# Second stage of an attention and feed-forward kernel: seven products of quarters in place of eight

## The chip, the cores and the metric

The kernel runs on one core of a Trainium2 chip. The metric is the device time of one execution in microseconds (us), the median of several runs. The profile is of one execution; its engines are PE (TensorE matmul), PEld (its weight loads), DVE (VectorE), ACT (ScalarE), POOL (GpSimd) and SP (SyncE, which issues DMAs here).

## The reference

A decayed attention over 2 batches, 8 heads, 768 positions and 64 channels gives x of 1536 tokens by 512. Then come a normalization and two feed-forward stages in float32:

```python
xn = x / np.sqrt(np.mean(x * x, axis=-1, keepdims=True) + 1e-06) * rms_g
g = xn @ w_gate                                  # 512 x 1536
y = (g * (1.0 / (1.0 + np.exp(-g))) * (xn @ w_val)) @ w_out
h = np.maximum(np.maximum(y @ w1, y @ w2), y @ w3)   # 512 x 768 each
out = h @ w_out2
```

Call the line of y the first stage, the last two lines the second.

## The kernel before

**Tiles.** Tokens are columns, cut into NBLK=3 blocks j of 512. The contraction of 512 is cut into KD=4 slices of 128. The width of the first stage is 12 tiles f of 128, that of the second 6. `feed_forward` (L427) goes through a list of steps (stage, group, j, f): within a group of f (groups1 = 4, 2, 2, 2, 2; groups2 = 2, 2, 2) over the three blocks j, and within j over the f. A step makes a hidden tile (`hidden1` L384: the products pg and pv, sigmoid, two multiplications; `hidden2` L396: three products pw0 to pw2, one ACT copy, two DVE maxima), cuts it (`split`), and while PE goes on, the step before it is multiplied by its rows of the output weight (`out1`, `out2`) into four PSUM banks `acc`. At a group's end `drain1` or `drain2` adds these to a sum in SBUF; at the end of the last group of the first stage `drain1` also cuts y into yh and yl. PSUM has 8 banks of 128x512, all from one pool.

**Float32 by three products.** `mm3` (L336) does each 128x128 by 128x512 product as three matmuls: high by high, high weight by low data, low weight by high data. A high part is a cast to fp32r on ACT, the low part source minus high: `split` (L349) puts the cast (hh, L350) on ACT and the subtraction (hl, L351) on POOL.

**Weights.** A weight tile of 512 columns (a unit: name g, v, o of the first stage; 1, 2, 3, p of the second; and f) arrives as 64-bit words in the tile `wraw` by a DMA from SP, three in flight. `make_unit` (L142) turns it into wh and wl over three calls, each of which advances three units at once: ACT does an absolute value and a scaling of the raw words (L173, L174); a call later DVE does three operations (L153, L155, L157: `W`) and POOL one integer addition (L159); a call later ACT casts wh (L148) and POOL subtracts wl (L149). All instructions stand in the order in which the Python code issues them. `gap` (L323) is called after each 6 matmuls of the products and the output products, and makes every fourth of these calls a `make_unit` in both stages' main part. So what stands behind what in an engine's queue is set by where `gap` falls.

```python
        pos["gap"] += 1
        if (pos["gap"] + 5) % (2 if pos["step"] < groups1[0] else 4) == 0:
            make_unit()
```

Of the kernel before, what the change touches and what calls it, by code (L numbers as in the profile page):

```python
# [18 lines left out]
P = 128  # L19
# [7 lines left out]
def tile_decay_attention_swiglu_maxout(  # L27
# [23 lines left out]
    NB = 512  # L51
    WBUFS = 12
# [12 lines left out]
    wpools = [wp]  # L65

# [42 lines left out]
    unit_list = [(nm, f) for f in range(F1) for nm in "gvo"] + [(nm, f) for f in range(F2) for nm in "123p"]  # L109
    groups1, groups2 = [4, 2, 2, 2, 2], [2, 2, 2]  # L110
    group_of = {}
    for n0, groups, names in ((0, groups1, "gvo"), (len(groups1), groups2, "123p")):
        f0 = 0
        for g_, n_ in enumerate(groups):
            group_of.update({(nm, f): n0 + g_ for nm in names for f in range(f0, f0 + n_)})
            f0 += n_
    steps = []
    for stage_, groups in ((1, groups1), (2, groups2)):
        f0 = 0
        for g_, n_ in enumerate(groups):  # L120
# [21 lines left out]
    def make_unit():  # L142

        if len(stage2):
            key, W, at = stage2.pop(0)
            wh = wpools[at].tile([P, 512], F32R, tag="wh", name="wh")
            wl = wpools[at].tile([P, 512], F32R, tag="wl", name="wl")
            nc.scalar.copy(out=wh, in_=W.bitcast(F32))  # L148
            nc.gpsimd.tensor_tensor(out=wl, in0=W.bitcast(F32), in1=wh.bitcast(F32), op=ALU.subtract)  # L149
            units[key] = (wh, wl)  # L150
        if len(stage1):
            key, W, at, lo, hi = stage1.pop(0)
            nc.vector.tensor_scalar(out=W.bitcast(F32), in0=W.bitcast(F32), scalar1=LEAST, scalar2=MOST,  # L153
                                    op0=ALU.max, op1=ALU.min)
# [10 lines left out]
        if first_use[key] <= pos["step"] + 6 and at < len(wpools) and room[at]:  # L165
            load_to(pos["made"] + (3 if pos["step"] else 1))
            room[at] -= 1
            held[key] = at
            pos["made"] += 1
            t = raws.pop(key).rearrange("p k (f w) -> p (k f) w", w=2)  # L170
            lo, hi = t[:, :, 0], t[:, :, 1]
            W = wp.tile([P, 512], I32, tag="W", name="W", bufs=3)
# [150 lines left out]
    def gap():  # L323
# [17 lines left out]
    def proj(ps, unit, bh, bl):  # L341
        wh, wl = unit
        for kk in range(KD):
            ks = slice(kk * P, (kk + 1) * P)
# [10 lines left out]
    yb = {}  # L355

    def drain1(acc, g, j):
        if g == 0:
# [3 lines left out]
            return  # L362
        for m in range(KD):
            nc.vector.tensor_tensor(out=acc_sb[j][:, m, :], in0=acc[m], in1=acc_sb[j][:, m, :], op=ALU.add)
        if g == len(groups1) - 1:
            yh = act.tile([P, KD, NB], F32R, tag="xh", name="yh", bufs=3)
            yl = act.tile([P, KD, NB], F32R, tag="xl", name="yl", bufs=3)
            for m in range(KD):
                split(yh[:, m, :], yl[:, m, :], acc_sb[j][:, m, :])
            yb[j] = (yh, yl)  # L370

    def drain2(acc, g, j):
        if g == 0:
            acc_sb[j] = act.tile([P, KD, NB], F32, tag="acc", name="acc_sb", bufs=3)
        for t in range(KD):
            if g == 0:
                nc.scalar.copy(out=acc_sb[j][:, t, :], in_=acc[t])
                continue
            nc.vector.tensor_tensor(out=acc_sb[j][:, t, :], in0=acc[t], in1=acc_sb[j][:, t, :], op=ALU.add)
            if g == len(groups2) - 1:  # L380
                r0 = j * NB + t * P
                nc.sync.dma_start(out=out[r0:r0 + P, :], in_=acc_sb[j][:, t, :])

    def hidden1(f, j):  # L384
# [4 lines left out]
        proj(pv, units["v", f], bh, bl)  # L389
# [5 lines left out]

    def hidden2(f, j):  # L396
        bh, bl = yb[j]
        ps = []
        for i in range(3):
            pw = bank(f"pw{i}")  # L400
            proj(pw, units["123"[i], f], bh, bl)
            ps.append(pw)
        m1 = act.tile([P, NB], F32, tag="sg", name="m1", bufs=1)
        nc.scalar.copy(out=m1, in_=ps[0])
        nc.vector.tensor_tensor(out=m1, in0=ps[1], in1=m1, op=ALU.max)  # L405
        nc.vector.tensor_tensor(out=m1, in0=ps[2], in1=m1, op=ALU.max)
        return m1
# [9 lines left out]
    def out2(acc, f, f0, f1, hh, hl):  # L417
        wh, wl = units["p", f]
        for t in range(NB // P):
            ts = slice(t * P, (t + 1) * P)  # L420
            nc.tensor.matmul(out=acc[t], lhsT=hh[:, ts], rhs=wh, start=f == f0, stop=False)  # L421
            nc.tensor.matmul(out=acc[t], lhsT=hh[:, ts], rhs=wl, start=False, stop=False)  # L422
            nc.tensor.matmul(out=acc[t], lhsT=hl[:, ts], rhs=wh, start=False, stop=f == f1)  # L423
            if t % 2:
                gap()

    def feed_forward():  # L427
        acc = []
        before = None
        for now in steps + [None]:  # L430
            if now:
                pos["step"] = steps.index(now)
                stage, g, j, f, f0, f1 = now
                if stage == 1 and g == 0 and f == f0:
# [7 lines left out]
                r = (hidden1 if stage == 1 else hidden2)(f, j)  # L442
                hh = act.tile([P, NB], F32R, tag="hh", name="hh")
                hl = act.tile([P, NB], F32R, tag="hl", name="hl")
                split(hh, hl, r)
            if before:
                stage, g, j, f, f0, f1, ph, pl = before
                if f == f0:
                    acc = [bank("acc") for _ in range(4)]
                (out1 if stage == 1 else out2)(acc, f, f0, f1, ph, pl)  # L450
                if f == f1:
                    (drain1 if stage == 1 else drain2)(acc, g, j)
                if j == NBLK - 1:
                    for nm in ("gvo" if stage == 1 else "123p"):
                        del units[nm, f]
                        room[held.pop((nm, f))] += 1
            if now:
                before = (*now, hh, hl)
# [64 lines left out]
```

## Time and profile before

| | us |
|---|---|
| median of 3 runs (lowest, highest) | 581.58 (581.4, 581.93) |
| the profiled execution | 582.03 |
| its span in the profile | 580.2 |
| PE busy in the span | 563.9 |
| DVE busy | 341.4 |
| ACT busy | 223.4 |
| POOL busy | 292.7 |
| mean granted TensorE clock | 0.996 |

The span is what the profiler saw of the core's instructions; the execution's own time holds what lies around it as well. Busy time is the time in which an engine ran an instruction, and PE's part of it holds all the kernel's matmuls. Tiles of the second stage are called pw, m, hh, hl and acc in the rows, those of the first pg, pv, sg, hh, hl and acc; the hidden tile of the second stage uses the buffer of sg.

### The profile page before, as it was taken

The page shows a single profiled execution, that of the slowest core. Times are in us where ns is not written, and L with a number is a line of the kernel's source. Part 1 is how long each engine was busy: PE and PEld are TensorE (multiplying, and loading weights), DVE is VectorE, ACT ScalarE, POOL GpSimd, SP SyncE. Part 2 cuts the span into 40 slices and gives each one's busy share as a digit, 9 for nine tenths or more (in the row PEclk, how much of TensorE's full clock was granted, in tenths as well). Part 3 has the DMA queues.
Part 4 walks back from the last instruction along what each step waited for, and adds up shares of the span by engine and source line. Part 5 has one row for each costly group of instructions (what it writes and reads, how often), then busy time and mean ns, then how long its engine had stood idle before and what let it go on. Part 6 is the DMA issues. An engine that isn't in the chain of part 4 may idle for free.

```text
span 580.2 us, 7727 instructions
## 1 busy us (share of the span) xinstructions
PE 563.9 (97%) x2970; PEld 466.5 (80%) x2970; DVE 341.4 (59%) x467; ACT 223.4 (38%) x422; POOL 292.7 (50%) x231
## 2 busy tenths in 40 slices
PE   7979898999999999999999999999999999999997
PEld 7868676888788888888888888888888888888885
DVE  6687996433556783775477388868732674321322
ACT  3656653432453642342253245553532533101100
POOL 2577988211356773365256257988741566110110
PEclk9998999999999999999999999999999999999999
DMA  9677554000033231132033022322321220000111
GB/s 213 169 194 193 143 163 128 1 2 0 2 108 110 73 108 37 36 104 78 0 111 105 4 72 73 109 74 73 108 73 37 69 77 2 0 0 1 74 72 73
DMA packets 64645, 44.54 MB, mean 77 GB/s; under 512 B 39264, under 2 KB 60768, under 8 KB 64608
## 3 DMA queue, kind: packets, MB, share of 16 engines
q1 hardware_dynamic: 63936, 44.05, 25.8%
q8 instruction: 23, 0.38, 0.3%
q14 instruction: 14, 0.11, 0.1%
q10 hardware_dynamic: 672, 0.01, 0.1%
HBM read 40.90 MB, written 3.15 MB: 76 GB/s over the span
## 4 chain that ended last, share of the span: by engine, by line
PE 87%; DVE 7%; DMA 2%; ACT 2%; issue 1%; SPq 0%; POOL 0%; DVEq 0%; ACTq 0%
PE pw L339 8%; PE pw L337 8%; PE pw L338 8%; PE acc L337 5%; PE pv L337 5%; PE pg L337 5%; PE pg L338 5%; PE pv L339 5%; PE acc L339 5%; PE pg L339 5%; PE acc L338 5%; PE pv L338 5%; PE acc L423 3%; PE acc L421 3%; PE acc L422 3%; PE px L244 2%
## 5 line engine op out<-in xcount | busy, mean ns | idle before, releaser
L149 POOL TENSOR_TENSOR wl<-W,wh 128x512 fp32r<-128x512 f32 x60 | 90.7, 1511 | 21.1 <-ACT wh L148 21.1
L351 POOL TENSOR_TENSOR hl<-sg,hh 128x512 fp32r<-128x512 f32 x36 | 47.3, 1314 | 101.3 <-ACT hh L350 98.4
L159 POOL TENSOR_TENSOR W<-W,wraw 128x512 int32<-128x512 int32 x60 | 80.1, 1335 | 17.9 <-DVE W L157 13.0
L157 DVE SCALAR_TENSOR_TENSOR W<-wraw,W 128x512 int32<-128x512 int32 x60 | 84.3, 1405 | 2.1
L337 PE MATMUL pw<-yh,wh 128*128 128x512 f32 x216 | 84.0, 389 | 0.0
L338 PE MATMUL pw<-yl,wh 128*128 128x512 f32 x216 | 84.0, 389 | 0.0
L339 PE MATMUL pw<-yh,wl 128*128 128x512 f32 x216 | 84.0, 389 | 0.0
L351 POOL TENSOR_TENSOR hl<-m,hh 128x512 fp32r<-128x512 f32 x18 | 23.3, 1294 | 102.3 <-ACT hh L350 102.3
L392 DVE TENSOR_TENSOR sg<-pg,sg 128x512 f32<-128x512 f32 x36 | 24.7, 687 | 60.2 <-ACT sg L391 60.2
L337 PE MATMUL pv<-xh,wh 128*128 128x512 f32 x144 | 57.1, 397 | 1.0 <-DVE x L300 1.0
L337 PE MATMUL pg<-xh,wh 128*128 128x512 f32 x144 | 58.0, 403 | 0.1
L148 ACT CAST wh<-W 128x512 fp32r<-128x512 f32 x60 | 37.2, 619 | 54.4 <-POOL W L159 54.3
L338 PE MATMUL pg<-xl,wh 128*128 128x512 f32 x144 | 56.7, 394 | 0.5 <-DVE xl L311 0.5
L339 PE MATMUL pg<-xh,wl 128*128 128x512 f32 x144 | 56.7, 394 | 0.3 <-POOL wl L149 0.3
L337 PE MATMUL acc<-hh,wh 128*128 128x512 f32 x144 | 56.9, 395 | 0.0
L350 ACT CAST hh<-sg 128x512 fp32r<-128x512 f32 x36 | 22.4, 622 | 88.9 <-DVE sg L393 88.9
L339 PE MATMUL pv<-xh,wl 128*128 128x512 f32 x144 | 56.2, 390 | 0.0
L339 PE MATMUL acc<-hh,wl 128*128 128x512 f32 x144 | 56.1, 390 | 0.0
L338 PE MATMUL acc<-hl,wh 128*128 128x512 f32 x144 | 56.1, 390 | 0.0
L338 PE MATMUL pv<-xl,wh 128*128 128x512 f32 x144 | 56.1, 390 | 0.0
L405 DVE TENSOR_TENSOR m<-pw,m 128x512 f32<-128x512 f32 x18 | 12.4, 691 | 70.6 <-PE pw L339 59.8
L153 DVE TENSOR_SCALAR W<-W 128x512 f32<-128x512 f32 x60 | 42.6, 710 | 9.2 <-POOL hl L351 4.8
(84 smaller groups left out, 1063.3 us busy)
## 6 DMA issues: line engine op xcount, KB each, us to landing
wraw<-in_moe_w_out_dram SPq DMA_DIRECT2D x18, 512.0 KB, 3.3
wraw<-in_moe_w_dram SPq DMA_DIRECT2D x18, 512.0 KB, 3.5
wraw<-in_moe_w_gate_dram SPq DMA_DIRECT2D x12, 512.0 KB, 3.6
wraw<-in_moe_w_val_dram SPq DMA_DIRECT2D x12, 512.0 KB, 3.6
kn<-in_k_dram SPq DMA_DIRECT2D x12, 256.0 KB, 4.0
qn<-in_q_dram SPq DMA_DIRECT2D x12, 256.0 KB, 4.4
vn<-in_v_dram SPq DMA_DIRECT2D x12, 256.0 KB, 4.7
out_dram<-acc_sb SPq DMA_DIRECT2D x12, 256.0 KB, 2.1
```

The costliest lines, as they stand in the source:

```text
L148: nc.scalar.copy(out=wh, in_=W.bitcast(F32))
L149: nc.gpsimd.tensor_tensor(out=wl, in0=W.bitcast(F32), in1=wh.bitcast(F32), op=ALU.subtract)
L153: nc.vector.tensor_scalar(out=W.bitcast(F32), in0=W.bitcast(F32), scalar1=LEAST, scalar2=MOST, op0=ALU.max, op1=ALU.min)
L157: nc.vector.scalar_tensor_tensor(out=W, in0=hi, scalar=-0x40000000, in1=W, op0=ALU.bitwise_and, op1=ALU.bitwise_or)
L159: nc.gpsimd.tensor_tensor(out=W, in0=W, in1=lo, op=ALU.add)
L337: nc.tensor.matmul(out=out, lhsT=wh, rhs=xh_, start=first, stop=False)
L338: nc.tensor.matmul(out=out, lhsT=wh, rhs=xl_, start=False, stop=False)
L339: nc.tensor.matmul(out=out, lhsT=wl, rhs=xh_, start=False, stop=last)
L350: nc.scalar.copy(out=dst_h, in_=src)
L351: nc.gpsimd.tensor_tensor(out=dst_l, in0=src, in1=dst_h.bitcast(F32), op=ALU.subtract)
L392: nc.vector.tensor_tensor(out=sg, in0=pg, in1=sg, op=ALU.mult)
L421: nc.tensor.matmul(out=acc[t], lhsT=hh[:, ts], rhs=wh, start=f == f0, stop=False)
```

## The change

The first stage's steps stay, except for their end. The second stage is written anew, as a list of pieces.

**Seven products for eight.** For a pair of f (three pairs g) and each of w1, w2, w3 (i), the blocks j=0 and j=1 and the two halves of the contraction make a two by two matrix of quarters, as do the pair of f and the halves of the weight. Their product takes eight products of quarters (6 matmuls of 128x512 each). The change does it in Strassen's way, in Winograd's form, with seven. They need sums of quarters of y (s1 to s4, made once) and of the weights (T1, T2, T3, per pair and made in place in `W` by four DVE subtractions of 128x256, L174, then cast and cut like any unit: 18 more units of cast and low half). Block j=2 stays plain: four pieces of 6 matmuls per pair and weight. So a pair and weight takes 11 pieces, 66 matmuls, where it took 72.

**Banks.** The products 1, 6, 7 and 4 accumulate one after another into one bank `p`, 5 and 3 into a bank `r`, 2 into `q`. Between them ACT copies the state of the bank to SBUF (`held_back`: c1, u2, m5), and DVE adds that copy to another bank (`add_max`): for i=0 one addition, for i=1, 2 an addition and a maximum of two SBUF tiles. `just_max` is one ACT copy (i=0) or one DVE maximum with a bank.

**Placing.** `first_stage` runs out1 of (f=11, j=1) early, in the middle of pv of (f=10, j=2) (`early`), and its `drain1` leaves two of four sums in PSUM; `sums_of_quarters` puts six pieces of work into `later`, and each `gap` pops one. T1, T2 of the first pair and the units 1, 2, 3 of it are made in the first stage. The last out1 (f=11, j=2) stands behind two pieces of the second stage (`second_stage`). `gap` makes a unit after pieces 5, 2 and 7, and after every second token tile of out2, which now stands once per pair, for all three j.

```diff
+    unit_list = [(nm, f) for f in range(F1) for nm in "gvo"]
+    unit_list += [("1", 0), ("1", 1), None, ("T1", 0), ("T1", 1), ("2", 0), ("2", 1), None, ("T2", 0), ("T2", 1),
+                  ("3", 0), ("3", 1)]
...
+            elif key and key[1] % 2 == 0:
+                a, b = W.bitcast(F32), words[key[0][1], key[1] + 1].bitcast(F32)
+                for o, x, y in ((a[:, :HF], b[:, :HF], a[:, :HF]), (b[:, :HF], b[:, HF:], b[:, :HF]),
+                                (b[:, HF:], b[:, HF:], a[:, :HF]), (a[:, HF:], a[:, HF:], b[:, HF:])):
+                    nc.vector.tensor_tensor(out=o, in0=x, in1=y, op=ALU.subtract)
...
+        keep = g == len(groups1) - 1 and j == 1
+        for m in (0, 2, 1, 3) if keep else range(KD):
+            nc.vector.tensor_tensor(out=acc[m] if keep and m < 2 else y[:, m, :], in0=acc[m], in1=y[:, m, :], op=ALU.add)
...
+        if keep:
+            sums_of_quarters(list(acc), y)
+            return
...
+        def cut(nm, k, src, eng):
+            h_, l_, o = Y[nm]
+            nc.scalar.copy(out=h_[:, o + k, :], in_=src)
+            lower(eng, h_[:, o + k, :], l_[:, o + k, :], src)
+
+        def one(k):
+            s3[k] = wpools[1].tile([P, NB], F32, tag=("wh", "wl")[k], name="sums")
+            nc.vector.tensor_tensor(out=s3[k], in0=y0[:, k, :], in1=ps[k], op=ALU.subtract)
+            nc.vector.tensor_tensor(out=ps[k], in0=ps[k], in1=y[:, 2 + k, :], op=ALU.add)
+            cut("s1", k, ps[k], nc.vector)
+
+        def two(k):
+            s4 = wpools[1].tile([P, NB], F32, tag=("wh", "wl")[k], name="sums")
+            nc.vector.tensor_tensor(out=ps[2 + k], in0=ps[k], in1=y0[:, k, :], op=ALU.subtract)
+            nc.vector.tensor_tensor(out=s4, in0=y0[:, 2 + k, :], in1=ps[2 + k], op=ALU.subtract)
+            cut("s2", k, ps[2 + k], nc.vector)
+            cut("s4", k, s4, nc.gpsimd)
+
+        def three(k):
+            cut("s3", k, s3[k], nc.gpsimd)
+            cut("22", k, y[:, 2 + k, :], nc.gpsimd)
+
+        for k in range(2):
+            later.extend([lambda k=k: one(k), lambda k=k: two(k), lambda k=k: three(k)])
...
+    def add_max(ps, c, i, key, n):
+
+        if i == 0:
+            nc.vector.tensor_tensor(out=hidden_tile(key, n), in0=ps, in1=c, op=ALU.add)
+            return
+        nc.vector.tensor_tensor(out=c, in0=ps, in1=c, op=ALU.add)
+        nc.vector.tensor_tensor(out=hid[key], in0=hid[key], in1=c, op=ALU.max)
+        if i == 2:
+            halves(key)
...
+        if n == 1:
+            ps_of[at, "p"] = p = bank("p")
+            product(p, u0, 0, Y["11"], True)
+            ps_of[at, "c1"] = held_back(p, "wh")
...
+        elif n == 6:
+            product(ps_of[at, "p"], t1, 1, Y["s2"], False)
+            ps_of[at, "u2"] = held_back(ps_of[at, "p"], "wl")
...
+        elif n == 2:
+            q_ = bank("q")
+            product(q_, u0, 1, Y["12"], True)
+            add_max(q_, ps_of.pop((at, "c1")), i, (0, 0), 2)
...
+        gap(n in (5, 2, 7))
...
+        work = [(first, 1), (first, 2), halve, finish, (first, 5), (first, 6), (second, 1), (first, 3), (first, 7),
+                (second, 2), (first, (0, 0)), (first, 4), (second, 5), (first, (0, 1)), (second, 6), (first, (1, 0)),
+                (second, 3), (first, (1, 1)), (second, 7), (second, (0, 0)), (second, (0, 1)), (second, 4),
+                (second, (1, 0)), (second, (1, 1))]
+        for g in range(F2 // 2):
+            for i in range(3):
+                if g or i == 2:
+                    work += [((g, i), n) for n in (1, 5, (0, 0), 6, 2, (0, 1), 3, 7, (1, 0), (1, 1), 4)]
+                if g and i == 0:
+                    work.append(lambda g=g: out2(g - 1))
+        work.append(lambda: out2(F2 // 2 - 1))
```

**Place 1: POOL at the end of the first stage, before.** hl_3415 is the low half of the last hidden tile of the first stage, (f=11, j=2); wl_3442 and W_3447 belong to units of the second stage; yl_3516 are the low halves of y of block 2.

```order
L351 TENSOR_TENSOR hl_3415<-sg_3410,hh_3414 128x512 [waits Activation_49]
L149 TENSOR_TENSOR wl_3442<-W_3353,wh_3441 128x512 [waits Activation_49]
L159 TENSOR_TENSOR W_3447<-W_3447,wraw_3305 128x512 [waits DMAHW2_49,DVE_49,Activation_49]
L351 TENSOR_TENSOR hl_3496<-m1_3491,hh_3495 128x512 [waits Activation_49]
L351 TENSOR_TENSOR yl_3516<-acc_sb_1939,yh_3515 128x512 [waits Activation_49] x4
```

And now: hl_3449 is that same low half. xl1, xl2 and al hold the sums of quarters, W_3423 is a unit of the second pair, yl_3511 are the low halves of y of block 2.

```order
L390 TENSOR_TENSOR xl2_3368<-sums_3397,xh2_3367 128x512 [waits DVE_49,Activation_49]
L390 TENSOR_TENSOR xl1_3366<-sums_3377,xh1_3365 128x512 [waits Activation_49]
L390 TENSOR_TENSOR al_3370<-acc_sb_1671,ah_3369 128x512 [waits Activation_49]
L390 TENSOR_TENSOR xl2_3368<-sums_3437,xh2_3367 128x512 [waits DVE_49,Activation_49]
L390 TENSOR_TENSOR xl1_3366<-sums_3426,xh1_3365 128x512 [waits Activation_49]
L390 TENSOR_TENSOR al_3370<-acc_sb_1671,ah_3369 128x512 [waits Activation_49]
L169 TENSOR_TENSOR W_3423<-W_3423,wraw_3229 128x512 [waits DMAHW0_49,DVE_49]
L383 TENSOR_TENSOR hl_3449<-sg_3444,hh_3448 128x512 [waits PE_49,Activation_49,Pool_49]
L383 TENSOR_TENSOR yl_3511<-acc_sb_1942,yh_3510 128x512 [waits Activation_49] x4
```

The last hidden tile's low half stands behind six low halves of sums and behind the addition for W_3423.

**Place 2: DVE at the same place, before.** sg_3410 is the last hidden tile of the first stage, acc_sb_1668 the sum of block 1, m1_3491 the first hidden tile of the second stage.

```order
L364 TENSOR_TENSOR acc_sb_1668<-acc_3276,acc_sb_1668 128x512 [waits PE_49]
L364 TENSOR_TENSOR acc_sb_1668<-acc_3277,acc_sb_1668 128x512 [waits PE_49]
L153 TENSOR_SCALAR W_3353<-W_3353 128x512 [waits Activation_49,Pool_49]
L155 TENSOR_SCALAR W_3353<-W_3353 128x512 [waits DVE_49]
L157 SCALAR_TENSOR_TENSOR W_3353<-wraw_3255,W_3353 128x512 [waits DMAHW1_49,DVE_49]
L392 TENSOR_TENSOR sg_3410<-pg_3376,sg_3410 128x512 [waits Activation_49,Pool_49]
L393 TENSOR_TENSOR sg_3410<-pv_3389,sg_3410 128x512 [waits DVE_49,PE_49]
L153 TENSOR_SCALAR W_3447<-W_3447 128x512 [waits Activation_49,Pool_49]
L155 TENSOR_SCALAR W_3447<-W_3447 128x512 [waits DVE_49]
L157 SCALAR_TENSOR_TENSOR W_3447<-wraw_3305,W_3447 128x512 [waits DMAHW2_49,DVE_49]
L405 TENSOR_TENSOR m1_3491<-pw1_3456,m1_3491 128x512 [waits PE_49,Activation_49]
L406 TENSOR_TENSOR m1_3491<-pw2_3469,m1_3491 128x512 [waits DVE_49,PE_49]
```

And now: acc_3301 to acc_3304 are the banks of the early out1 with the sums of block 1, sg_3444 the hidden tile (11, j=2), q_3479 the second piece of the second stage.

```order
L437 TENSOR_TENSOR sums_3426<-acc_sb_1337,acc_3302 128x512
L438 TENSOR_TENSOR acc_3302<-acc_3302,acc_sb_1671 128x512
L390 TENSOR_TENSOR xl1_3366<-acc_3302,xh1_3365 128x512 [waits Activation_49]
L443 TENSOR_TENSOR acc_3304<-acc_3302,acc_sb_1337 128x512
L444 TENSOR_TENSOR sums_3437<-acc_sb_1337,acc_3304 128x512 [waits DVE_49]
L390 TENSOR_TENSOR xl2_3368<-acc_3304,xh2_3367 128x512 [waits Activation_49]
L465 TENSOR_TENSOR sg_3444<-pg_3390,sg_3444 128x512 [waits Activation_49]
L466 TENSOR_TENSOR sg_3444<-pv_3414,sg_3444 128x512 [waits DVE_49,PE_49]
L553 TENSOR_TENSOR m_3486<-q_3479,c_3477 128x512 [waits PE_49,Activation_49]
L163 TENSOR_SCALAR W_3423<-W_3423 128x512
L165 TENSOR_SCALAR W_3423<-W_3423 128x512 [waits DVE_49]
L167 SCALAR_TENSOR_TENSOR W_3423<-wraw_3229,W_3423 128x512 [waits DMAHW0_49,DVE_49]
```

The sums of the second quarter tile stand ahead of the last hidden tile's two multiplications, and the conversion of W_3423 stands behind the addition m_3486, which waits for PE's q_3479. The first matmul into q_3479 waits for the row of xl2 from acc_3304.

**Place 3: ACT where pair 0 ends and pair 1 begins, before.** The step of the second stage that makes m1_3491 (its copy and cast), then the cut of y and units.

```order
L404 COPY m1_3491<-pw0_3434 128x512 [waits PE_49,Pool_49]
L350 CAST hh_3495<-m1_3491 128x512 [waits DVE_49]
L350 CAST yh_3515<-acc_sb_1939 128x512 [waits DVE_49] x4
L148 CAST wh_3532<-W_3447 128x512 [waits Pool_49]
L173 ACTIVATE W_3542<-wraw_3445 128x512 [waits DMAHW4_49,Activation_49]
L174 ACTIVATE wraw_3445<-wraw_3445 128x512
L148 CAST wh_3571<-W_3482 128x512 [waits Pool_49]
L173 ACTIVATE W_3581<-wraw_3480 128x512 [waits DMAHW5_49,Activation_49]
```

And now: hh2_3835, hh2_3853 and hh2_3864 are casts of finished hidden tiles of pair 0 (m_3568, m_3670, m_3614), c_3875 and c_3884 the copies of the banks p and r of the first two products of pair 1.

```order
L157 CAST wh_3822<-W_3747 128x512 [waits Pool_49]
L197 ACTIVATE W_3832<-wraw_3745 128x512 [waits DMAHW5_49,Activation_49]
L198 ACTIVATE wraw_3745<-wraw_3745 128x512
L382 CAST hh2_3835<-m_3568 128x512 [waits DVE_49]
L382 CAST hh2_3853<-m_3670 128x512 [waits DVE_49]
L382 CAST hh2_3864<-m_3614 128x512 [waits DVE_49]
L577 COPY c_3875<-p_3868 128x512 [waits PE_49]
L577 COPY c_3884<-r_3877 128x512 [waits PE_49]
```

The copy that lets piece 6 of pair 1 overwrite its bank stands behind the casts of three hidden tiles, which wait for DVE. DVE reaches m_3670 and m_3614 there only behind three operations on W_3784:

```order
L555 TENSOR_TENSOR c_3739<-p_3723,c_3739 128x512 [waits PE_49]
L556 TENSOR_TENSOR m_3568<-m_3568,c_3739 128x512 [waits DVE_49]
L163 TENSOR_SCALAR W_3784<-W_3784 128x512 [waits Activation_49]
L165 TENSOR_SCALAR W_3784<-W_3784 128x512 [waits DVE_49]
L167 SCALAR_TENSOR_TENSOR W_3784<-wraw_3596,W_3784 128x512 [waits DMAHW4_49,DVE_49]
L564 TENSOR_TENSOR m_3670<-p2_3839,m_3670 128x512 [waits PE_49]
L564 TENSOR_TENSOR m_3614<-p_3723,m_3614 128x512 [waits PE_49]
```

## Rows read from the trace of the kernel before

**Rows 1.** The page, part 1: engine, busy us (share of the span) xinstructions.

```profile
PE 563.9 (97%) x2970; PEld 466.5 (80%) x2970; DVE 341.4 (59%) x467; ACT 223.4 (38%) x422; POOL 292.7 (50%) x231
```

**Rows 2.** The page, part 2: 40 slices, PE busy and granted clock in tenths.

```profile
PE   7979898999999999999999999999999999999997
...
PEclk9998999999999999999999999999999999999999
```

**Rows 3.** One window of the second stage: busy us of each engine, PEclk, DMA share, GB/s.

```profile
500.00:550.00 50.00, 50.00 (x223) 41.39 (x222) 12.36 (x18) 5.44 (x10) 5.16 (x4) 1.00 0.06 21
```

**Rows 4.** The tile pw, then the timeline's end: start us, us, engine, line.

```profile
L337 PE MATMUL pw<-yh,wh x216: 389/389/389, 377.7 to 570.1; 128*128 128x512 f32 x108
...
575.83 0.39 PE L422 MATMUL acc<-wl,hh 128*128 128x512 f32 x1
...
576.06 0.39 PE L423 MATMUL acc<-wh,hl 128*128 128x512 f32 x1
```

**Rows 5.** Groups by line and shape: busy us, mean ns of one, idle before.

```profile
L405 DVE TENSOR_TENSOR m<-pw,m 128x512 f32<-128x512 f32 x18 | 12.4, 691 | 70.6 <-PE pw L339 59.8 <-ACT m L404 10.7
...
L391 ACT ACTIVATE sg<-pg 128x512 f32<-128x512 f32 x36 | 21.3, 591 | 43.3 <-PE pg L339 43.3
...
L350 ACT CAST hh<-m 128x512 fp32r<-128x512 f32 x18 | 11.2, 622 | 73.0 <-DVE m L406 73.0
...
L404 ACT COPY m<-pw 128x512 f32<-128x512 f32 x18 | 10.4, 580 | 33.1 <-PE pw L339 33.1
...
L173 ACT ACTIVATE W<-wraw 128x512 f32<-128x512 f32 x60 | 40.1, 668 | 0.0
...
L351 POOL TENSOR_TENSOR hl<-m,hh 128x512 fp32r<-128x512 f32 x18 | 23.3, 1294 | 102.3 <-ACT hh L350 102.3
...
L159 POOL TENSOR_TENSOR W<-W,wraw 128x512 int32<-128x512 int32 x60 | 80.1, 1335 | 17.9 <-DVE W L157 13.0 <-ACT m L404 1.6 <-ACT wraw L174 1.6
```

**Rows 6.** Lines 311, 153, 155, 157 on DVE: duration min/median/max in ns.

```profile
L311 DVE TENSOR_TENSOR xl<-x,xh x4: 681/693/967, 112.9 to 148.2; 128x512 fp32r<-128x512 f32 x4
...
L153 DVE TENSOR_SCALAR W<-W x60: 411/419/1516, 24.9 to 484.6; 128x512 f32<-128x512 f32 x60
...
L155 DVE TENSOR_SCALAR W<-W x60: 426/428/1421, 25.3 to 485.0; 128x512 int32<-128x512 int32 x60
...
L157 DVE SCALAR_TENSOR_TENSOR W<-wraw,W x60: 691/1726/1811, 26.5 to 485.5; 128x512 int32<-128x512 int32 x60
```

**Rows 7.** Timeline near 362 us, DVE and POOL alone: start us, us, line.

```profile
361.11 1.38 DVE L153 TENSOR_SCALAR W<-W 128x512 f32<-128x512 f32 x1
...
362.16 1.47 POOL L149 TENSOR_TENSOR wl<-W,wh 128x512 fp32r<-128x512 f32 x1
...
362.52 1.39 DVE L155 TENSOR_SCALAR W<-W 128x512 int32<-128x512 int32 x1
...
363.95 1.67 DVE L157 SCALAR_TENSOR_TENSOR W<-wraw,W 128x512 int32<-128x512 int32 x1
```

**Rows 8.** Timeline, DVE and ACT: four free operations, two dependent ones, a handover.

```profile
371.66 1.88 DVE L364 TENSOR_TENSOR acc_sb<-acc,acc_sb 128x512 f32<-128x512 f32 x3
...
400.94 0.69 DVE L405 TENSOR_TENSOR m<-pw,m 128x512 f32<-128x512 f32 x1 [1.78 <-ACT m L404]
...
401.74 0.69 DVE L406 TENSOR_TENSOR m<-pw,m 128x512 f32<-128x512 f32 x1
...
402.46 0.62 ACT L350 CAST hh<-m 128x512 fp32r<-128x512 f32 x1 [1.61 <-DVE m L406]
```

**Rows 9.** Windows of half a microsecond in the first stage: columns as in Rows 3.

```profile
40.50:41.00 0.50, 0.00 (x0) 0.00 (x0) 0.50 (x3) 0.21 (x1) 0.22 (x1) 1.00 1.28 283
...
43.00:43.50 0.50, 0.50 (x5) 0.40 (x4) 0.50 (x1) 0.18 (x2) 0.50 (x1) 0.77 1.05 239
...
43.50:44.00 0.50, 0.50 (x3) 0.40 (x2) 0.50 (x1) 0.50 (x2) 0.27 (x1) 0.50 1.05 238
...
46.50:47.00 0.50, 0.50 (x5) 0.49 (x4) 0.50 (x1) 0.00 (x0) 0.50 (x1) 0.82 0.00 0
```

More of the change, by code (lines that the diff above doesn't have):

```diff
@@ L362, in drain1 @@
             return
-        for m in range(KD):
[L364 to L382, printed above, removed]
@@ L415, in out1, with first_stage @@
                 gap()
[L417 to L427, printed above, removed]
+    def first_stage():
         acc = []
         before = None
-        for now in steps + [None]:
+        for now in steps:
             if now:
                 pos["step"] = steps.index(now)
-                stage, g, j, f, f0, f1 = now
-                if stage == 1 and g == 0 and f == f0:
+                g, j, f, f0, f1 = now
+                if g == 0 and f == f0:
                     while attn_q and attn_q[0][0] <= 6 + 4 * j:
@@ L446, in feed_forward @@
[L446 to L456, printed above, removed]
@@ L457, in feed_forward, with finish @@
-            if now:
-                before = (*now, hh, hl)
+                if now == steps[-1]:
+                    halve = lambda: split(hh, hl, r)
+                else:
+                    split(hh, hl, r)
+                if before and not early:
+                    finish()
+                def finish(now=now, hh=hh, hl=hl):
+                    g, j, f, f0, f1 = now
+                    if f == f0:
+                        acc[:] = [bank("acc") for _ in range(4)]
+                    out1(acc, f, f0, f1, hh, hl)
+                    if f == f1:
+                        drain1(acc, g, j)
+                    if j == NBLK - 1:
+                        free(("o", f))
@@ new lines, in first_stage, with free, product @@
+            before = now
+        return halve, finish
+    def free(*keys):
+        for key in keys:
+            del units[key]
+            room[held.pop(key)] += 1
+    hid = {}
+    parts = {}
+    def product(ps, unit, half, x, first):
+        wh, wl = unit
+        xh_, xl_, o = x
+        for k in range(2):
+            ks = slice((2 * half + k) * P, (2 * half + k + 1) * P)
+            for n, (w, r) in enumerate(((wh, xh_), (wh, xl_), (wl, xh_))):
+                nc.tensor.matmul(out=ps, lhsT=w[:, ks], rhs=r[:, o + k, :], start=first and k == 0 and n == 0,
+                                 stop=k == 1 and n == 2, skip_group_check=True)
@@ new lines, in second_stage @@
+    def second_stage(halve, finish):
+        first, second = (0, 0), (0, 1)
+        work = [(first, 1), (first, 2), halve, finish, (first, 5), (first, 6), (second, 1), (first, 3), (first, 7),
[9 more added lines that the diff above has]
+        work.append(lambda: out2(F2 // 2 - 1))
+        for w in work:
+            if callable(w):
+                w()
+            else:
+                piece(*w[0], w[1])
```

225 lines of the change are left out of this document (173 added, 52 removed).

## The prediction, made before the change was run

> **What bounds the kernel now.** I read the page's totals first [rows 1]: PE is busy 97% of the span. The slices say where the other 3% is [rows 2]: from the seventh slice on PE shows 9 throughout, at the full granted clock, until the tail. One window of the second stage confirms it [rows 3]: 50.00 of 50 us, clock 1.00, while DVE is busy 12.36 and POOL 5.16 us. So a matmul fewer in the second stage is worth a matmul's pitch, as long as nobody else becomes late. The pitch comes from the second stage's length [rows 4]: the first matmul into pw starts at 377.7, the last into acc at 576.06, with 864 of the stage and 12 of the last out1 between: 198.36 / 875 = 0.2267 us.
>
> **What it removes.** Per pair and weight 66 matmuls for 72, nine times: 54 x 0.2267 = **-12.24 us**. The order shows this literally, so that the change doesn't do what it says is out. SP issues the same 60 weight loads in another order; with PE, not DMA, bound in that stage (DMA share 0.06 [rows 3]) I cost this at nothing. After the last matmul the path (one DVE addition, one store) is unchanged: nothing.
>
> **Prices of what it adds.** An addition with a bank: 0.69 us [rows 5], one that depends on the operation before it 0.80 from start to start, free ones (1.88 - 0.69) / 2 = 0.60 [rows 8]. Handing over from DVE to ACT costs 0.03 (401.74 + 0.69 to 402.46 [rows 8]). Copy of a bank 0.58, cast 0.62, sigmoid 0.59, raw weight 0.67, low half on POOL 1.29, integer addition 1.34 [rows 5]. Low half on DVE 0.68 to 0.97 [rows 6]. Three operations of a unit on DVE: 0.42 + 0.43 + 0.69 = 1.54 at least, 2.57 with the third at its median [rows 6]. Not in the trace are: an addition from one bank to another (between 0.60 and 0.80, I take 0.69, the nearest shape); a 128x256 subtraction in SBUF (between 0.42 [rows 6] and 0.97, I take 0.42, since it has half the columns of the 0.69); a maximum of two SBUF tiles (0.69 to 0.97, I take 0.69). Eighteen units more on POOL are 18 x 1.3 = 23 us beside PE's 810 x 0.2267 = 184; they cost only where PE waits for one.
>
> **First place: the last out1 (f=11, j=2), places 1 and 2 of the order.** Let zero be the start of the early out1 of (11, j=1). PE then has, by the pitch, out1 until 2.72, the rest of pv until 4.08, pg and pv of (11, 2) until 9.52, out1 of (10, 2) until 12.24, product 1 (p) until 13.60, product 2 (q) until 14.96; the second matmul of the last out1, which needs hl_3449, is due at 15.19.
>
> DVE: four additions end at 4.15. First quarter tile: difference and sum to 5.37, ACT cast to 6.0, low half to 6.73; the hidden tile of (10, 2), whose sigmoid stands behind that cast, to 8.13. Two differences to 9.53, cast 10.16, low half 10.9. Second tile: difference and sum to 12.1; on ACT three casts and two operations of a unit stand ahead, so its cast ends at 13.65, the low half at 14.4, the difference at 15.0. That frees p's bank: PE is 15.05 - 12.24 = 2.8 late. The next difference 15.8, cast 16.4, low half 17.2 free q's bank: q runs from 17.2 to 18.56, **3.6 late**.
>
> Then POOL decides. Its queue has ahead of hl_3449 six low halves of sums (the last three depend on DVE at 15.8 and end at 20.95) and the integer addition for W_3423. DVE does that unit's three operations only behind m_3486, which needs q: 18.56 plus copy and addition is 20.04; plus 0.3 + 0.45 + 0.7, and the last of the six to leave POOL, 22.5. Addition 23.9, hl_3449 25.15. PE's second matmul, due at 15.19, starts 25.15: **+10.0 us**, the 3.6 included. Of this a part is built in, however early the sums are: from q's end 0.2 + 0.69 + 1.5 + 1.3 + 1.3 = 5.0. Cover for it would be PE work between q and the last out1; there is none.
>
> **The clock.** PE would stand some 6 us there. The nearest row is in the first stage [rows 9]: at 40.5 PE runs nothing, the granted level falls to 0.50 (the 1.2 GHz level) within 43.0 to 43.5 (mean 0.77) and is back within 46.5 to 47.0 (0.82): from about 43.27 to 46.68, 3.4 us at half speed, 1.7 us of work lost. I add **+1.7**; the bounds are 0 and 3.4.
>
> **Second place: the change of pairs, 0 to 1, place 3 of the order.** Product 6 of (1, 0) adds into bank p and so waits for the copy c_3875. On ACT this stands behind three casts; they wait for DVE's m_3670 and m_3614, and these stand behind three operations for W_3784, at a time when POOL has a unit as well. In such a stretch of the trace DVE's operations take 1.38, 1.39 and 1.67 us, together 4.44 and not 1.54 [rows 7]. With these the copy ends so late that product 6, due 34 pieces x 6 x 0.2267 = 46.24 after the last out1, starts at 48.9: **+2.7**; with 1.54 it would be in time, so the bounds are 0 and 2.7.
>
> All other places that I walked through keep slack, the smallest 0.2 us (pair 1 to 2): nothing, up to +1.
>
> **Sum.** 582.03 - 12.24 + 10.0 + 2.7 + 1.7 = 584.19 for the profiled execution, which lies 0.45 above the median of the runs: **583.7 us**.
>
> **A rule against the change.** In the trace DVE's operation on two SBUF tiles runs 0.68 to 0.97 [rows 6], and L157 mostly 1.73 where POOL is at work: while POOL's low half runs from 362.16 to 363.63, L155 beside it takes 1.39 [rows 7]. The Trainium skill ("SBUF — State Buffer", section "SBUF: two separate sides") says why: DVE and GpSimd share one port pair as an exclusive lock, held for a whole instruction, so a DVE operation with two SBUF inputs blocks against a GpSimd operation that reads SBUF; the trace agrees, with 1.73 for 0.69. By the rule the change's new maxima and subtractions, all with two SBUF inputs, would block as well, while additions from a bank would not; the last rival gives the time, 588.6.
>
> **Rivals.**
> - *The sums are early enough.* Some 18 dependent steps stand at 0.80 in my walk; at the 0.60 of free ones [rows 8] the chain gains 3.6 us, the banks come in time and only the built-in 5.0 stays, if POOL's six halves end before its queue is asked too: 582.03 - 12.24 + 5.0 + 2.7 + 1.7 = 579.2, less 0.45: 578.7. It decides at whether q starts before about 14. For it: DVE is idle much of the time beside this place; against it: the steps are chained through ACT.
> - *The clock stays.* Then 584.19 - 1.7 - 0.45 = 582.0, no change. For it: PE isn't wholly idle for all of the stretch but works between p, q and out1; against it [rows 9], where the level fell while PE was at work again.
> - *DVE becomes the bound at out2 of pair 1* (on the slower side still). There 12 banks take PE 12 x 6 x 0.2267 = 16.3 us, and DVE has 12 additions x 0.69, two units x 2.57 and 8 subtractions: at 0.42 16.8 us, which eight banks of 1.36 us each cover, at 0.97 21.2, so 4.9 more: 583.7 + 4.9 = 588.6. For it: POOL's share of the port; against it: half the columns. It decides from a subtraction of some 0.6 us on.
>
> **How the numbers follow.** Chances: forecast 0.42, early sums 0.29, clock stays 0.15, DVE bound 0.14. A measurement of this kernel can tell about 0.2%, 1.16 us, from no change: faster is below 580.42, slower above 582.74. The forecast's own range is 581.0 to 586.5 (the change of pairs without its 2.7; the clock at 3.4 and the 1 of the other places): 0.07 within 0.2%, 0.35 slower. Early sums give 0.28 faster and 0.01 same; the clock's case 0.02, 0.11 and 0.02; DVE's 0.14 slower. Together 0.30 faster, 0.19 same, 0.51 slower. The range goes from 577.0 (early sums, with part of the 2.7 at the change of pairs gone) to 588.0; what is left out is half of the DVE case and the tails, about 0.18.
>
> **What would show it.** In the profile after: 810 matmuls of pieces and out2 where 864 stood, at the same pitch; q's first matmul 3 to 4 us after p could have ended; one gap of PE of 5 to 7 us before the second matmul of the last out1, ended by POOL's hl, with W_3423's addition just before it; a stretch at half clock behind it; a second gap of 2 to 3 us at product 6 of pair 1's first weight, ended by an ACT copy. If the first gap is under 6 us in all, or the change of pairs has none, I am wrong by those terms; if DVE's subtractions take over 0.6 us and PE waits for DVE in out2 of pair 1, the last rival holds.

## The result and the profile after

The changed kernel takes 586.06 us (median of 6 runs, 584.64 to 586.49) against 581.75 in the same measurement (581.39 to 583.86): ratio 1.006, 95% interval 1.0039 to 1.0081. It is slower, as forecast, by 4.3 us where the prediction had 2.1. The profiled execution took 586.49 us, its span is 584.7.

The totals, the slices of PE and the clock, and the window that answers to [rows 3], from the page and the windows of the kernel after:

```profile
PE 558.1 (95%) x2916; PEld 458.3 (78%) x2916; DVE 392.8 (67%) x542; ACT 246.4 (42%) x464; POOL 319.9 (55%) x251
...
PE   8989899999999999999999999959998999999997
...
PEclk9999998999999999999999999989999999999999
...
500.00:550.00 50.00, 48.44 (x213) 39.46 (x212) 40.94 (x55) 19.21 (x35) 30.94 (x23) 1.00 0.13 43
```

54 matmuls are gone (2916 for 2970), and PE has got less busy, while DVE is busy 41 us in that window where it was 12 [rows 3], and POOL 31 where it was 5. PE, full from the seventh slice on in [rows 2], now has a hole (the 5; the clock's row has an 8 in the same slice) and a smaller one four slices on (the 8). What PE waited for from the end of the first stage on, in the view of waits (us in total, times, the longest):

```profile
PE acc L368 <- POOL hl L383: 5.0, 2, 4.7
PE p L533 <- ACT c L577: 3.2, 3, 1.6
PE p L533 <- DVE acc L443: 1.6, 1, 1.6
PE acc L367 <- ACT hh L382: 0.8, 1, 0.8
PE q L533 <- DVE xl L390: 0.4, 1, 0.4
```

Before, there was none. Most of them are at the joins, the places where PE needs the result of another engine's queue, that the prediction walked through and priced: the hidden tile's low half, the two banks p and q, the copy at the change of pairs 0 to 1. Not priced, or priced at nothing, were the 0.8 for the cast hh, 0.3 of the 5.0 for the low half of the tile before, and two of the three copies c.

To add it up, both traces are taken from one event on, the first matmul into pg of (f=11, j=2), called S, since the first stage ahead of it varies from run to run (last section). L is the start of the last matmul:

```profile
370.14 0.39 PE L367 MATMUL pg<-xh,wh 128*128 128x512 f32 x1
...
580.56 0.39 PE L639 MATMUL acc<-wh,hl 128*128 128x512 f32 x1
```

Before, S is 369.54 and L 576.06 [rows 4]: 206.52 us for 912 matmuls, 911 pitches of 0.2267, so nothing was lost. After, 858 matmuls need 857 x 0.2267 = 194.28, and S to L takes 210.42: **16.14 us are lost**. 12.24 less and 16.14 more is +3.9; S itself is 0.6 later, which makes the 4.5 by which the spans differ.

The largest loss, line by line, from the timeline after (start, duration):

```profile
380.67 0.50 PE L533 MATMUL p<-yh,wh 128*128 128x512 f32 x1 [1.62 <-DVE acc L443]
...
382.74 0.49 PE L533 MATMUL q<-yh,wh 128*128 128x512 f32 x1 [0.41 <-DVE xl L390]
...
384.52 0.69 DVE L553 TENSOR_TENSOR m<-q,c 128x512 f32<-128x512 f32 x1
...
385.04 1.27 POOL L390 TENSOR_TENSOR al<-acc_sb,ah 128x512 fp32r<-128x512 f32 x1
385.13 1.47 DVE L163 TENSOR_SCALAR W<-W 128x512 f32<-128x512 f32 x1
...
387.09 0.69 DVE L167 SCALAR_TENSOR_TENSOR W<-wraw,W 128x512 int32<-128x512 int32 x1
387.86 1.27 POOL L169 TENSOR_TENSOR W<-W,wraw 128x512 int32<-128x512 int32 x1 [1.55 <-DVE W L167]
389.09 1.26 POOL L383 TENSOR_TENSOR hl<-sg,hh 128x512 fp32r<-128x512 f32 x1
390.41 0.80 PE L368 MATMUL acc<-hl,wh 128*128 128x512 f32 x1 [4.71 <-POOL hl L383]
```

The reader sees the chain of the order come true: q, the addition m, three operations on W_3423, POOL's integer addition, the low half, PE. The second matmul of the last out1 was due 49 pitches behind S, at 381.25, and starts at 390.41: 9.16 late. The clock behind it, in windows of 5 us (last but two column PEclk):

```profile
385.00:390.00 5.00, 0.50 (x1) 0.19 (x1) 2.71 (x4) 0.14 (x1) 3.45 (x4) 0.96 0.00 0
390.00:395.00 5.00, 4.59 (x11) 3.64 (x12) 2.08 (x3) 1.28 (x3) 2.27 (x3) 0.50 0.30 105
395.00:400.00 5.00, 5.00 (x21) 4.08 (x20) 4.42 (x4) 2.88 (x5) 4.65 (x4) 0.86 0.00 0
```

The granted level is 0.50 (1.2 GHz) until about 396.47 (0.86 is 0.14 short of 1 over 5 us, so 1.4 to 1.5 us at half). From 390.41 on that is 6.06 us of work at half speed, 3.03 lost.

### The profile page after: what moved, and what is told of

Its sections match the earlier page's. It is cut to its first block, busy times and chain, and to the rows that moved or that the text cites. A ratio compares the mean times of both kernels' runs of the same rounds, so it can differ in the third digit from the quotient of the medians.

```text
span 584.7 us, 7768 instructions
## 1 busy us (share of the span) xinstructions
PE 558.1 (95%) x2916; PEld 458.3 (78%) x2916; DVE 392.8 (67%) x542; ACT 246.4 (42%) x464; POOL 319.9 (55%) x251
## 4 chain that ended last, share of the span: by engine, by line
PE 75%; DVE 14%; ACT 4%; issue 2%; DMA 2%; POOL 2%; SPq 0%; DVEq 0%; POOLq 0%; ACTq 0%
PE p L533 13%; PE acc L367 5%; PE acc L368 5%; PE acc L369 5%; PE pv L367 5%; PE pg L367 5%; PE pv L369 5%; PE pv L368 5%; PE pg L368 5%; PE pg L369 5%; PE r L533 3%; PE acc L639 2%; PE acc L637 2%; PE acc L638 2%; DVE W L167 2%
## 5 line engine op out<-in xcount | busy, mean ns | idle before, releaser
L158 POOL TENSOR_TENSOR wl<-W,wh 128x512 fp32r<-128x512 f32 x78 | 113.1, 1450 | 59.5 <-ACT wh L157 59.5
L167 DVE SCALAR_TENSOR_TENSOR W<-wraw,W 128x512 int32<-128x512 int32 x60 | 80.1, 1335 | 2.1
L157 ACT CAST wh<-W 128x512 fp32r<-128x512 f32 x78 | 48.3, 620 | 70.0 <-POOL W L169 61.8
L368 PE MATMUL acc<-hl,wh 128*128 128x512 f32 x144 | 57.6, 400 | 5.0 <-POOL hl L383 5.0
L367 PE MATMUL acc<-hh,wh 128*128 128x512 f32 x144 | 58.1, 404 | 0.8 <-ACT hh L382 0.8
L165 DVE TENSOR_SCALAR W<-W 128x512 int32<-128x512 int32 x60 | 44.4, 740 | 2.1
L197 ACT ACTIVATE W<-wraw 128x512 f32<-128x512 f32 x60 | 40.3, 671 | 2.6 <-POOL wl L158 2.6
L466 DVE TENSOR_TENSOR sg<-pv,sg 128x512 f32<-128x512 f32 x36 | 24.9, 692 | 23.3 <-PE pv L369 21.6
L198 ACT ACTIVATE wraw<-wraw 128x512 int32<-128x512 uint32 x60 | 39.8, 664 | 0.0
L383 POOL TENSOR_TENSOR hl<-m,hh 128x512 fp32r<-128x512 f32 x18 | 26.4, 1492 | 20.9 <-ACT hh L382 20.9
```

Of the source, the lines that this page charges most:

```text
L197: nc.scalar.activation(out=W.bitcast(F32), in_=hi.bitcast(F32), func=AF.Abs)
L367: nc.tensor.matmul(out=out, lhsT=wh, rhs=xh_, start=first, stop=False)
L368: nc.tensor.matmul(out=out, lhsT=wh, rhs=xl_, start=False, stop=False)
L383: nc.gpsimd.tensor_tensor(out=dst_l, in0=src, in1=dst_h.bitcast(F32), op=ALU.subtract)
```

## The experiments

The theory: the 54 matmuls do give 12.24 us, and what is lost is queue joins, each movable. The standing rival: DVE and POOL, in each other's way as in [rows 7], have become the bound of the stage, so that a wait taken away comes back at the next piece. Each run is compared with the kernel before by the ratio of times, and with the kernel after by its trace from S on.

**The conversion later.** For the first pair and weight a unit is made behind product 6, which follows the last out1, and not behind product 2, which is ahead of it.

```diff
-        gap(n in (5, 2, 7))
+        gap(n in (5, 7) or n == (6 if at == (0, 0) else 2))
```

> Theory (POOL's queue): in the changed kernel the low half that the last out1 waits for ends at 390.35, behind the integer addition for a weight, which itself waits for DVE. With that unit's conversion made after the last out1, the low half follows the six low halves of the sums, which end at 386.3, and ends at about 387.6: 2.8 us earlier. So 586.06 - 2.8 = 583.3, less up to 3.0 more if the shorter idle time no longer lets the clock fall. Rival (the sums are late for a reason of DVE's, and the wait only changes its name): the low half ends where it did, 586 within 0.5.

Measured: 581.86 us, ratio to before 1.0004 (0.9989 to 1.0018). The low half now follows the sums:

```profile
385.98 1.26 POOL L383 TENSOR_TENSOR hl<-sg,hh 128x512 fp32r<-128x512 f32 x1
387.30 0.50 PE L368 MATMUL acc<-hl,wh 128*128 128x512 f32 x1 [1.89 <-POOL hl L383]
```

From S to this matmul it takes 17.45 us where it took 20.27: 2.8 less, as expected. The clock stays at 1.00 behind the shorter wait. Part of it came back: product 4 waits 0.8 for DVE, whose four subtractions for T3 now lie there and take 4.97 us for the 1.7 of free ones. 4.2 of the at most 5.8 us came by the median: the place of one unit's conversion in the queues was worth the whole loss against the kernel before.

**The last out1 later.**

```diff
-        work = [(first, 1), (first, 2), halve, finish, (first, 5), (first, 6), (second, 1), (first, 3), (first, 7),
-                (second, 2), (first, (0, 0)), (first, 4), (second, 5), (first, (0, 1)), (second, 6), (first, (1, 0)),
+        work = [(first, 1), (first, 2), halve, (first, 5), (first, 6), (second, 1), (first, 3), finish, (first, 7),
+                (second, 2), (first, 4), (second, 5), (second, 6), (second, 3), (second, 7), (first, (0, 0)),
...
```

> Theory (nothing stands between product 2 and the last out1 to cover POOL's queue): with four pieces of the seven products (5, 6, the other weight's 1, and 3) ahead of the last out1, 5.4 us of PE's work lie over the wait; of the 9.2 us that PE was late only the 2.5 of the two banks stay, and the clock does not fall: 586.06 - 6.7 - 3.0 = 576.4 (range 575.5 to 579). Rival (DVE and POOL share a port and are the bound at this place): the low half comes later by as much, and little is gained, 584 or more.

Measured: 582.66 us, ratio 1.0009 (0.9995 to 1.0023), a miss by 6 us. The cover did what it should: the low half's wait is 0.73 for 4.71, and the clock does not fall. But the reordered list put the second weight's products 5, 6 and 3 next to each other, without plain pieces between, and PE meets a new wait of 3.09 for a bank copy, from the timeline of this run:

```profile
399.12 2.87 POOL L158 TENSOR_TENSOR wl<-W,wh 128x512 fp32r<-128x512 f32 x2
...
400.60 0.67 ACT L197 ACTIVATE W<-wraw 128x512 f32<-128x512 f32 x1 [3.08 <-POOL wl L158]
...
402.20 0.58 ACT L577 COPY c<-r 128x512 f32<-128x512 f32 x1
...
402.83 0.50 PE L533 MATMUL r<-xh,wh 128*128 128x512 f32 x1 [3.09 <-ACT c L577]
```

ACT's raw operation needs a buffer that POOL's low half frees, POOL stands until 399.12 at the four yl of block 2 (5.50 us from 393.65 on), and the copy stands behind the raw operation. A wait came back at a later piece, as the rival has it; that it is one more join and not a bound is shown only by the combined version below, which has the same work and not this wait.

**PE kept at work.** The 24 matmuls are extra work on a finished tile, whose result nobody reads.

```diff
+        if f == F1 - 1 and f0 < f and len(done) == 1:
+            fill = bank("fill")
+            y_ = Y["11"][0]
+            for n_ in range(24):
+                nc.tensor.matmul(out=fill, lhsT=wh[:, 0:P], rhs=y_[:, 0, :], start=n_ == 0, stop=n_ == 23)
```

> 24 matmuls of a finished tile into a bank that nobody reads stand ahead of the last out1, so PE works through the time in which it waited; everything else is as in the changed kernel, and the low half comes at the same time. Theory (the clock fell because PE stood idle): no stretch at 0.50 behind the wait, and 3.0 us less, 583.1. Rival (the low clock has another cause, or the work left at half speed lay beside something else): 586 within 0.7, or later.

Measured: 584.01 us, ratio 1.0031 (1.0016 to 1.0045). The same stretch of windows:

```profile
385.00:390.00 5.00, 5.00 (x24) 4.14 (x23) 3.83 (x5) 1.23 (x3) 3.45 (x3) 1.00 0.00 0
390.00:395.00 5.00, 4.57 (x21) 3.46 (x20) 2.62 (x4) 1.77 (x3) 2.75 (x3) 1.00 0.29 105
395.00:400.00 5.00, 5.00 (x24) 4.14 (x23) 4.71 (x6) 3.21 (x7) 5.00 (x5) 1.00 0.00 0
```

The clock stays. The low half comes as late as before (20.36 us behind S, 20.27 after), and from there to L it takes 187.33 us for 190.15: 2.8 us are the clock's, shown by themselves; the run's median is 2.05 lower than that of the kernel after.

**The casts later** at the change of pairs: the two pops of `later` behind pieces (1, 1) and 4 of the third weight are left to the next pair's pieces.

```diff
-        if later:
+        if later and pop:
             later.pop(0)()
...
-        gap(n in (5, 2, 7))
+        gap(n in (5, 2, 7), i < 2 or g == 2 or n not in ((1, 1), 4))
```

> At the change of pairs (0 to 1 and 1 to 2) the casts of the last two hidden tiles are issued behind the copies of the next pair's first two products. Theory (ACT's order makes the bank copy late): PE's waits of 1.6 and 0.4 us there go, 586.06 - 2.0 = 584.0. Rival (PE then waits for DVE or POOL a piece later, since DVE is the one that is behind): 586 within 0.6.

Measured: 583.74 us, ratio 1.0029 (1.0016 to 1.0043); from the low half's matmul to L 187.90 us for 190.15, 2.25 less. Of PE's three waits for the copy c one is left, 1.3 behind out2 of pair 1, and a new one of 0.4 for DVE:

```profile
PE p L533 <- ACT c L577: 1.3, 1, 1.3
...
PE p L533 <- DVE m L553: 0.4, 1, 0.4
```

**The make behind out2** (the third wait for c alone).

```diff
-                gap(t % 2 == 1)
+                gap(t % 2 == 1 and not (g == 1 and j == 2 and t == 3))
...
-        gap(n in (5, 2, 7))
+        gap(n in (5, 2, 7) or at == (2, 1) and n == (0, 1))
```

> The changed kernel with the last make of out2 for pair 1 moved behind a later piece, and nothing else. Theory (the bank copy stands on ACT behind the cast and the raw operations of a unit, and that cast behind DVE's four subtractions): PE's wait of 1.1 us behind out2 goes, 586.06 - 1.1 = 585.0. Rival (the copy would wait for DVE's additions in any case): 586 within 0.5, the wait stays.

Measured: 585.91 us, ratio 1.0061 (1.0042 to 1.0079), by its median no different from the kernel after. The trace shows the part: two waits for c, 2.0 us, where there were three, 3.2, and from the low half's matmul to L 188.66 us for 190.15. The wait goes; that the time of the whole gets shorter by it the runs do not show.

**All of it**, in another order of the first pieces: products 5 and 6 and the second weight's 1 ahead of the last out1, no conversion until it is issued, plain pieces between the products as in the change. The edits of the casts and of out2's make are in it as well.

```diff
+        work = [(first, 1), (first, 2), halve, (first, 5), (first, 6), (second, 1), finish, (first, 3), (first, 7),
+                (second, 2), (first, 4), (first, (0, 0)), (second, 5), (first, (0, 1)), (second, 6), (first, (1, 0)),
...
+        if at == (0, 0):
+            make = n in (7, (0, 1), (1, 0), (1, 1))
+        if at == (0, 1):
+            make = n in (2, 7)
```

> The parts that worked, together, and the cover of the last out1 in another order: products 5 and 6 and the other weight's 1 stand ahead of it, no unit is converted until it is issued, the plain pieces of block 2 stay spread between the products, the casts at the change of pairs come behind the bank copies, and the last make of out2 for pair 1 is moved behind a later piece. Theory (all that the change gave back are queue joins, and each can be moved): of PE's lost 16.1 us behind the last pg of the first stage, 6.7 of the low half's wait, 3.0 of the clock, 2.3 of the copies at the change of pairs and 1.1 behind out2 go; the two banks' 2.5 stay: 586.06 - 13.1 = 573 (571.5 to 576). Rival (DVE and POOL are the bound of the stage through their shared port, so PE meets them again at the next piece): 579 or more, with new waits of PE for DVE or ACT in the second stage.

Measured: 576.81 us, ratio 0.9906 (0.9887 to 0.9924); S to L 199.56 us, 5.28 lost where 16.14 were. PE's waits from there on:

```profile
PE p L533 <- DVE acc L443: 1.6, 1, 1.6
PE p L533 <- DVE c L555: 1.1, 1, 1.1
PE q L533 <- DVE xl L390: 0.4, 1, 0.4
PE p L533 <- DVE m L553: 0.4, 1, 0.4
PE acc L368 <- POOL hl L383: 0.3, 1, 0.3
```

From S to L that is 10.9 of the 13.1 expected; two new waits for DVE's additions (1.1 and 0.4) are most of the rest. By the median it is 9.25, with 1.2 us more behind the last matmul (last section). The rival, 579 or more, falls, though new waits for DVE came, as it has them: they took back some 2 us of the 13.1. DVE and POOL are no bound of the stage.

**Sums early.** On DVE each low half of a sum is issued behind the next difference, so that ACT's cast has time; one conversion moves away from the additions.

```diff
-            cut("s1", k, ps[k], nc.vector)
...
+            nc.scalar.copy(out=h_[:, o + k, :], in_=ps[2 + k])
+            h1, l1, o1 = Y["s1"]
+            lower(nc.vector, h1[:, o1 + k, :], l1[:, o1 + k, :], ps[k])
             nc.vector.tensor_tensor(out=s4, in0=y0[:, 2 + k, :], in1=ps[2 + k], op=ALU.subtract)
-            cut("s2", k, ps[2 + k], nc.vector)
+            lower(nc.vector, h_[:, o + k, :], l_[:, o + k, :], ps[2 + k])
...
-        gap(n in (5, 2, 7))
+        make = n in (5, 2, 7)
+        if at == (0, 0):
+            make = n in (7, (0, 1), (1, 0))
+        if at == (0, 1):
+            make = n in (2, 7, (1, 0))
```

> The combined version with two more edits. The low halves of the sums are issued on DVE behind the next difference, so that DVE does not wait for each cast of ACT; and one conversion of a unit is moved away from in front of the additions of the second weight's products. Theory (the two banks come late because DVE waits some 0.65 us for each of four casts): PE's waits for the banks p and q, 1.6 and 0.4 us, shrink to under 0.5 together, and the wait of 1.1 for DVE's addition goes: 576.8 - 2.5 = 574.3 (573.5 to 575.5). Rival (DVE's own work is the bound there): both bank waits stay within 0.3, 576.8 within 0.8.

Measured: 573.91 us (573.58 to 575.99), ratio 0.9856 (0.9835 to 0.9877). S to L is 197.60 us, 3.32 lost. What is left of the waits, and a window of the second stage:

```profile
PE p L538 <- DVE xl L390: 1.7, 1, 1.7
PE p L538 <- DVE m L558: 0.4, 1, 0.4
PE acc L368 <- POOL hl L383: 0.3, 1, 0.3
...
500.00:550.00 50.00, 50.00 (x223) 41.38 (x222) 37.02 (x52) 16.81 (x31) 24.83 (x19) 1.00 0.09 32
```

Half a miss: the wait for q and the 1.1 are gone (which of the two edits took away the 1.1 no run tells), the one for p is not, it only has another releaser (the low half now reads p's bank last). Of the 2.9 us by which it lies below the combined version, 2.0 are between S and L; for the rest see the last section. It is the fastest of all, 1.4% below the kernel before, and PE is as full in that window as in [rows 3], with DVE three times as busy.

## Why the prediction was right, and where it was off

- **The matmuls, -12.24.** Right: the pitch is unchanged (223 matmuls in the 50 us of the last window, as in [rows 3]), and the sums early come out 8.9 us shorter from S to L than before (197.60 against 206.52), which leaves 3.32 of the 12.24 for the waits shown there.
- **The last out1, +10.0.** 9.16. From the start of the early out1 (366.06), p starts at 14.61 (15.05 in the walk), q at 16.68 (17.2), the low half's matmul at 24.35 (25.15). The walk was too slow by 0.4 at p, 0.5 at q and 0.9 at the addition behind q (it ends at 19.15, 20.04 in the walk), and that 0.9 goes through to the end. In part this is luck: behind the addition the prediction adds 0.3 + 0.45 + 0.7 to 20.04 and goes on from 22.5, where the sum is 21.5, so 1.0 us stands in it without a row. The trace has that microsecond: the first of the three operations took 1.47 beside POOL (from 385.13) where [rows 6] has 0.42. The sign was one gap of 5 to 7 us; it came as two, 0.8 for ACT's hh and 4.7 for hl, 6.0 in all from start to start, on the edge of the 6 below which the term was to be wrong. Of the 5.0 called built in, the conversion's move shows 2.8; the rest was not tested by itself.
- **The clock, +1.7.** The step that failed in size: 3.0 by the windows, 2.8 by the run that kept PE at work, for 1.7. I took the length of the one low stretch that the trace of before shows [rows 9], 3.4 us; this one is 6.8 long, 6.06 of it with work. The bounds, 0 and 3.4, held it.
- **The change of pairs, +2.7, other places nothing to +1.** 1.6 at pair 0 to 1, 0.4 at pair 1 to 2, 1.1 behind out2 of pair 1: 3.2 in all, at the predicted kind of place (a copy behind casts or a cast and raw operations on ACT), less at the one named and more at two that I had let off with slack. At the one named the queues stand as walked: DVE's three operations, stretched beside POOL to 1.52, 1.40 and 1.67 much as in [rows 7], then the maxima, the casts, the copy, PE. Why that makes 1.6 and not 2.7 can't be told, since the prediction gives only the end of its walk there. The lines:

```profile
436.80 1.52 DVE L163 TENSOR_SCALAR W<-W 128x512 f32<-128x512 f32 x1
...
438.36 1.40 DVE L165 TENSOR_SCALAR W<-W 128x512 int32<-128x512 int32 x1
...
439.79 1.67 DVE L167 SCALAR_TENSOR_TENSOR W<-wraw,W 128x512 int32<-128x512 int32 x1
...
441.38 1.27 DVE L564 TENSOR_TENSOR m<-p,m 128x512 f32<-128x512 f32 x2
...
441.84 0.39 PE L533 MATMUL p<-yh,wl 128*128 128x512 f32 x1
...
442.08 1.22 ACT L382 CAST hh<-m 128x512 fp32r<-128x512 f32 x2 [4.09 <-DVE m L564]
...
443.21 0.58 ACT L577 COPY c<-p 128x512 f32<-128x512 f32 x1
...
443.84 0.50 PE L533 MATMUL p<-xh,wh 128*128 128x512 f32 x1 [1.61 <-ACT c L577]
...
444.18 0.39 PE L533 MATMUL p<-xl,wh 128*128 128x512 f32 x1
```

- **What the three come to.** 9.16 + 3.03 + 3.17 = 15.36 of the 16.14. The 0.8 left lies in the three waits for c themselves: the 1.61 counts from the modelled end of the matmul before, but from 441.84 to 444.18, two pitches, it takes 2.34 us, 1.9 more than 2 x 0.2267. Read so from start to start, the three waits cost 1.9, 0.7 and 1.4, together 4.0 for the 3.2 of the view.
- **The sum.** +2.2 forecast for S to L, +3.9 measured: the out1 came 0.8 lower than forecast, the clock 1.3 and the copies 1.3 higher. What the spans differ by beyond it is the first stage's 0.6, which differs from run to run and belongs to no step.
- **Early sums** (578.7): it was to decide at whether q starts before 14; it starts at 16.68. **The clock stays** (582.0): it fell. **DVE the bound in out2** (588.6): its condition came true and its price did not. It was to hold from a subtraction of some 0.6 us on, and the eight subtractions in out2 of pair 1 take 2.60 and 3.03 us, 0.70 each; all 36 have a median of 0.43, a longest of 1.53 and a mean of 0.75. From the timeline and the lines' view after:

```profile
520.30 2.60 DVE L174 TENSOR_TENSOR W<-W 128x256 f32<-128x256 f32 x4
...
533.14 3.03 DVE L174 TENSOR_TENSOR W<-W 128x256 f32<-128x256 f32 x4
...
L174 DVE TENSOR_TENSOR W<-W x36: 412/426/1530, 319.3 to 535.7; 128x256 f32<-128x256 f32 x36
...
L556 DVE TENSOR_TENSOR m<-m,c x18: 691/694/1801, 405.0 to 562.5; 128x512 f32<-128x512 f32 x18
```

The maxima have 0.69 and 1.80. So they are blocked beside POOL as L157 was [rows 6, 7]: by their starts, 14 of the 36 subtractions begin while POOL runs an instruction, and 12 of these take 1.10 to 1.53, the other two begin in the last 0.3 us of POOL's and take 0.41 and 0.55; the 22 that begin beside an idle POOL take 0.41 to 0.43. The Trainium skill's rule ("SBUF — State Buffer", section "SBUF: two separate sides"), by which a DVE operation with two SBUF inputs waits out a GpSimd instruction that reads SBUF, agrees with the 1.53 and 1.80. Yet inside out2 PE waits for nobody, though DVE has some 18.4 us of work there for PE's 16.3; that the banks carry it over is likely, but no run tests it. What it does cost is the third copy: the four from 533.14 on stand in front of the cast that makes it late.

## What to carry to other kernels

When an edit takes work off a full engine and gives it to idle ones, walk the in-order queue of every helper at the few places where the full engine needs a result at once, and ask what stands ahead there that waits for the full engine itself: here one unit's conversion, put behind an addition that waited for product 2, stood ahead of the low half that PE needed next. Such joins are cheap to move, most by a line that says where a unit is made or a cast is popped, and moving them gave 12.8 of the 16.1 us lost; that a helper has idle time is no cover for a wrong place in its queue. Price an idle stretch of PE at its length plus the half-speed work behind it, and do not take that second part from a single low stretch: here there were some of 3.4 and some of 6.8 us.

## What the runs showed that I had not expected

- The low level lasted 6.8 us here (about 389.7 to 396.5), twice the 3.4 of [rows 9]; in the first stage of the conversion later and of the out2 make it lasted 6.8 too. An idle time of PE of 1.9 us at the same place (the conversion later) brought no fall, nor did one of 3.1 (the out1 later, 402.83); one of 4.7 did, in the change, the casts later and the out2 make.
- The first stage has such stretches of its own, not the same in each execution: one between 40 and 48 us in the traces of before, the conversion later, the out1 later and the make behind out2 (S at 369.54, 369.85, 369.39, 369.76), one at 96 to 100 in that of the change (370.14), one at either place in the combined version (371.21), three in PE kept at work (371.25), none in the casts later and the sums early (368.72 and 368.92). S goes with them, by up to 2.5 us, whatever the second stage does; parts of under 1 us can only be read from S on.
- In the two combined versions the span ends 4.2 us after DVE's last addition, in the change 3.0, though the same store of 256 KB stands behind it. It lands 3.2 us after its issue there, 2.0 in the change. No run tells why; it is left open.
